# A static schedule that models its load queue: a held weight transfer, copies kept on one engine, and re-measured durations

## Chip, cores and metric

One Trainium2 chip, one core. The metric is device time in microseconds (us) of one execution. The kernel before took 300.09 to 304.71 us. A profile shows one execution, and its span is 1.7 to 1.8 us shorter than that execution's time. The profile before is of a quick execution (300.43 us, 2.9 us under the median of 303.29).

## The reference

Attention over key blocks chosen by a gate, then an MLP on its output. Types are float32 in and out.

```python
# q, k, v: (4, 8, 768, 64).  w_in: (512, 2048), w_out: (2048, 512)
k_rep = k.reshape(B, H, 12, 64, D).mean(axis=3)            # one mean key for each 64-row block
gate  = einsum('bhsd,bhnd->bhsn', q, k_rep)                # where causal, else -1e9
mask  = own block | the 3 best blocks of gate, & causal
out   = softmax(where(mask, q @ k.T / 8, -1e9)) @ v
x     = out.transpose(0, 2, 1, 3).reshape(3072, 512)
return gelu_tanh(x @ w_in) @ w_out
```

## The kernel before

Heads go in pairs: pairs 0 to 3 are batch 0, 4 to 7 batch 1, and so on to 15. A pair needs loads of k, q and v, a gate (small float32 matmuls of q with the block-mean keys), a top-3 mask that a DMA transposes, and the attention itself. A batch then needs `s1` (MLP-up: 64 pairs of 512- and 256-column matmuls, each slice followed by a gelu on ScalarE) and `s2` (MLP-down, which needs all of w_out). The order is meant to overlap one batch's MLP with the next batch's gates and loads.

All of this is described as operations with a list of possible engines, a guessed duration, and dependencies. A greedy list scheduler in Python picks an engine and a place for each, once, when the program is built. On the chip the engines work through the chosen orders and wait on each other, so a wrong guess in the model becomes an order that stalls.

```python
class Plan:                                      # the scheduler, cut to its idea
    def solve(self):
        ...
        for op in cand:
            r = op.ready                          # when its dependencies end, in the model
            for e, d in op.engines.items():       # engine -> guessed us
                s = max(r, clock.get(e, 0.0))
                ests.append((s, s + d, e, op))
        first = min(x[0] for x in ests) + self.WINDOW
        # of those that can start first: the smallest prio, then the engine that ends it soonest
        ...

def load(p, key, held=None, prio=None):           # k, q, v of pair p, all issued by SyncE
    ...
    go = add({SP: 2.0 if dve else 1.0}, emit_t if dve else emit,
             [free_sd.get((key, p - (PV if key == "v" else PF))), held],
             prio=10 * p if prio is None else prio)          # the issue
    ld[key, p] = add({"DMA": 2.5 if dve else 1.8}, lambda _: None, [go],
                     prio=1000 * b + hp, lag=1.6)            # the landing, as modelled

free_sd["v", p] = ld["v16", p] = add({DVE: 0.47, ACT: 0.8}, emit, ...)   # cast of v
...
go  = add({SP: 1.2}, mask_dma, [sel], -50)                   # mask transpose, also on SyncE
m   = add({"XBAR": 0.8}, lambda _: None, [go], pr, lag=1.7)
mcs = [add({DVE: 0.25, ACT: 0.65}, mc(h), [m, old.get("s")], pr) for h in range(2)]  # mask copies
...
add({SP: 0.1}, out_e, [cp], -50)                             # output store, also on SyncE
...
# in the main sequence, at pair 5 (HP is 4):
w_ready["out"] = load_w("out", w_out16, moe_w_out, slice(0, DM), [issued["q", HP + 1]], 30)
```

For pairs 4 to 15, k and q come in as 128-byte records, already cut for VectorE's 32x32 transposes. w_out (2 MB, issued by GpSimd) comes in as 2048 records of 1024 bytes.

Two things in the built program matter that the model before does not have. First, SyncE's transfers take turns on eight semaphores (counters by which a transfer says that it has landed), as the operands in the trace show, so none is issued before the eighth transfer before it has landed. One load of k or q is four transfers, one of v is two. Second, an issue on SyncE can itself last long ("46.44 5.85 SPq" below), and the eight semaphores are not the reason: the fourth transfer of that line is issued from 48.52 to 52.29, while the eighth before it had landed at 47.15; the next transfer, of v, from 52.39 to 57.23, while the eighth before it had landed at 47.67. Of the single issues over 2 us, five of six fall while w_in or w_out is being loaded. What holds them stays open.

The softmax here doesn't subtract the row's maximum and nothing guards it: scores larger than these inputs give would overflow.

Of the kernel before, what the change touches and what calls it, by code (L numbers as in the profile page):

```python
# [8 lines left out]
FP32 = mybir.dt.float32  # L9
# [113 lines left out]
def kernel(  # L123
# [9 lines left out]
    nc = tc.nc  # L133
# [6 lines left out]
    HP = H // 2  # L140
    NPAIR = B * HP
    PF = 4
# [68 lines left out]
    issued = {}  # L211
    free_sd = {}

    def load(p, key, held=None, prio=None):
        b, hp = divmod(p, HP)

        def emit(_):
            sd = (iov if key == "v" else io).tile(
                [128, NC, 2, 64], FP32, tag=key, name=f"{key}_sd_{p}")
            for hh in range(2):  # L220
                nc.sync.dma_start(  # L221
                    out=sd[:, :, hh, :],
                    in_=SRC[key][b, 2 * hp + hh].rearrange(
                        "(c p) d -> p c d", p=128))
            T[key, p] = sd
        def emit_t(_):

            sd = io.tile([128, NC * 4, 32], FP32, tag=key, name=f"{key}_sd_{p}")
            for hh in range(2):
                for a in range(2):  # L230
                    nc.sync.dma_start(  # L231
                        out=sd[64 * hh + 32 * a:64 * hh + 32 * a + 32],
                        in_=SRC[key][b, 2 * hp + hh].rearrange(
                            "(t i) (a j) -> a i t j", i=32, j=32)[a])
            T[key, p] = sd
        dve = key != "v" and p >= HP
        go = add({SP: 2.0 if dve else 1.0}, emit_t if dve else emit,
                 [free_sd.get((key, p - (PV if key == "v" else PF))), held],
                 prio=10 * p if prio is None else prio)
        issued[key, p] = go  # L240
        ld[key, p] = add({"DMA": 2.5 if dve else 1.8},
                         lambda _: None, [go],
                         prio=1000 * b + hp, lag=1.6)

    def cast_v(p, old):
        b, hp = divmod(p, HP)

        def emit(eng):
            copy(eng, v16[p % NB][:, :, :, 0:64], T["v", p])
        free_sd["v", p] = ld["v16", p] = add(  # L250
            {DVE: 0.47, ACT: 0.8}, emit,
# [3 lines left out]
    def load_w(name, dst, src, cols, deps, prio):  # L255
        view = src.rearrange("(i p) f -> p i f", p=128)

        def emit(_):
            nc.gpsimd.dma_start(out=dst[:, :, cols], in_=view[:, :, cols])
# [76 lines left out]
    def pre(p):  # L336
# [51 lines left out]
        else:  # L388
            t = add({DVE: 0.95}, tr("k"),
# [15 lines left out]
            kcs = [add({DVE: 0.56, ACT: 0.73}, kc_all(h),  # L405
# [32 lines left out]
        else:  # L438
            t = add({DVE: 0.95}, tr("q"),
# [25 lines left out]
        gx = add({DVE: 0.32}, gm_e, [g], pr, gives=[("gt", p)])  # L465
# [18 lines left out]
        sel = add({DVE: 1.6}, sel_e, [gx, c_E["gates"], c_E["ones", i]], pr)  # L484
# [5 lines left out]
        else:  # L490
# [5 lines left out]
            q16s = [add({DVE: 0.56, ACT: 0.75}, q16(h), qcs + [old.get("s")],  # L496
# [26 lines left out]
        else:  # L523
            go = add({SP: 1.2}, mask_dma, [sel], -50)
            m = add({"XBAR": 0.8}, lambda _: None, [go], pr, lag=1.7)
# [6 lines left out]
            mcs = [add({DVE: 0.25, ACT: 0.65}, mc(h), [m, old.get("s")], pr)  # L532
# [18 lines left out]
    def table(key, deps, prio):  # L551
        if key not in tables:
# [6 lines left out]
            tables[key] = add({ACT: 1.5}, emit, deps, prio)  # L559
# [6 lines left out]
    def heads2(p):  # L566
# [81 lines left out]
        norms = [add({DVE: 0.72}, norm(p, h), pvs[h], base - 20,  # L648
# [18 lines left out]
    def turn_out(p, norms, base):  # L667
# [23 lines left out]
        if p >= HP + 2:  # L691
            go = add({SP: 1.2}, ot_dma, norms, -50)
            x = add({"XBAR": 0.8}, lambda _: None, [go], base - 20, lag=1.7)
        else:
            ot = add({PE: 0.33}, ot_e, norms, base + 50,
                     takes=("pre", ("oT", p)))
            x = add({DVE: 0.47, ACT: 0.7}, otc_e, [ot], base - 20,
# [3 lines left out]
    def heads(p):  # L701
# [5 lines left out]
        for h in range(2):  # L707
            pvs = []
            for gi, (ja, jb) in enumerate(groups):
# [30 lines left out]
                ex = add({ACT: 0.8}, ex_e,  # L740
# [33 lines left out]
            norms.append(add({DVE: 0.72}, norm(p, h), pvs, base - 20,  # L774
# [10 lines left out]
    def s1(b):  # L785
        for f in range(NF):
# [14 lines left out]
            def ge_e(_, f=f):  # L801
# [9 lines left out]
                add({ACT: 0.7}, ge_e,  # L811
# [4 lines left out]
    def s2(b):  # L816
        kind = "ops" if b < B - 1 else "tail"
        prev = None
        for ti in range(NC):
# [18 lines left out]
            cp = add({DVE: 0.6, ACT: 0.5}, cp_e, [mm], 1000 * b + 500,  # L838
# [42 lines left out]
    for p in range(HP, NPAIR):  # L881
# [6 lines left out]
        if p == HP + 1:  # L888
            w_ready["out"] = load_w("out", w_out16, moe_w_out, slice(0, DM),
                                    [issued["q", HP + 1]], 30)  # L890
            s2(0)
# [39 lines left out]
```

## Time and profile before

| | us |
|---|---|
| median of 4 runs beside the kernel after | 303.29 (302.52 to 304.36) |
| span of the profiled execution | 298.7 |
| TensorE busy / ScalarE / VectorE | 269.9 / 185.7 / 132.0 |

TensorE is 90% busy, but not evenly. The page's second part shows the span in 40 slices of 7.5 us (tenths of busy time; PEclk is the granted clock in tenths):

```profile
PE   7999999543699887995999999999999999999995
...
PEclk9999999957699999999899999999999999999999
DMA  9995999999998999999920222740002231000111
```

The eighth to eleventh digits (52 to 82 us) are the hole, and the clock drops in the ninth to eleventh. DMA is nearly full through the first twenty: up to there the loads lag behind what the engines could eat.

The stages can be cut by ScalarE's activation-table loads (gelu of batch 0, exp of batch 1, gelu of batch 1, exp of batch 2). Before the first is stage A. This is the windows view of the kernel before (stretch, its length, busy us and count of instructions of each engine, clock, DMA share, GB/s):

```profile
45.46:91.97 46.51, 31.53 (x206) 18.32 (x203) 17.36 (x53) 21.04 (x28) 1.90 (x3) 0.82 1.23 168
91.97:126.02 34.05, 29.93 (x311) 16.84 (x309) 25.59 (x69) 28.34 (x36) 10.16 (x23) 1.00 1.07 164
126.02:162.28 36.26, 32.35 (x211) 17.14 (x209) 23.48 (x85) 23.18 (x31) 0.81 (x1) 0.95 0.78 131
162.28:298.70 136.42, 132.78 (x1031) 73.96 (x1029) 37.14 (x120) 84.68 (x109) 20.55 (x48) 1.00 0.20 55
```

Call them B (MLP-up of batch 0), C (attention of batch 1), D (MLP-up of batch 1) and E (the rest). B lasts 46.5 us with TensorE busy for 31.5 us of it at clock 0.82; it is where the time is lost.

The two longest groups of waits of TensorE, before:

```profile
PE wide L792 <- ACT gT L805: 11.0, 2, 7.3
PE bank L449 <- DVE ksb L412: 7.7, 1, 7.7
```

And the timeline of the kernel before, around those waits (start, length, engine, line, operation, what it waited for before it in brackets):

```profile
46.19 1.17 POOL L259 DMA_DIRECT2D w_out<-in_moe_w_out_dram  x1
46.44 5.85 SPq L231 DMA_DIRECT2D q_sd<-in_q_dram  x4
...
63.01 0.98 DVE L372 STREAM_TRANSPOSE qT<-q_sd 128x768 f32<-128x768 f32 x1 [8.43 <-DMA q_sd<-in_q_dram]
...
64.12 0.76 PE L449 MATMUL bank<-qT,ksb 128*32 128x160 f32 x8 [7.67 <-DVE ksb L412]
...
72.25 1.31 SPq L510 DMA_TRANSPOSE mT<-madd  x1
...
75.65 0.72 ACT L202 COPY qT<-mT 12x640 f16<-12x640 f16 x1 [10.09 <-DMA mT<-madd]
...
77.26 13.14 PE L792 MATMUL wide<-xT,w_in 128*128 128x512 f16 x72 [7.30 <-ACT gT L805]
```

Read it as two chains. First: w_out is issued at 46.19, q of pair 5 at 46.44; q is not there until 63, so VectorE waits 8.43 us, and TensorE stands at the gate of pair 5 for 7.67 us. The bracket names ksb (the block-mean keys, spread out by VectorE for the gate's matmuls) because that multiply came last, but VectorE was itself waiting for q. Second: the mask transpose of pair 4 is issued only at 72.25, behind the loads up to k of pair 7 in SyncE's queue, though its input was ready at 52.7. A mask copy that the scheduler gave to ScalarE waits for it, the gelus stand behind that copy in ScalarE's order, and TensorE waits 7.30 us for a gelu to free its PSUM buffer.

The DMA records, counted from the raw trace of the kernel before (records per 2 us):

```text
window us     w_out (1024 B)   loads (128 B)
46 - 48             0              2346
50 - 52           385                63
52 - 54           293               288
54 - 56           357               354
58 - 60           353               354
w_out runs from 48.4 to 61.5
```

From 52 to 60 us the two flows get the same number of records, so w_out gets eight times the bytes. The Trainium skill ("DMA: Bandwidth & Descriptors", Queues, rings and completion order) says that each DMA engine goes round its queue rows packet by packet. A packet of that page holds several descriptors, and the trace shows single records, so it can't show the packets; equal shares agree with the page if the packets of both flows hold equally many. The number from the trace: the loads fall from about 1,170 records per us to about 180.

### The profile page before, as it was taken

To read this page: it belongs to the slowest core of one execution; us is meant where nothing else is said; L and a number is where in the kernel's file an instruction comes from. 1 tells how busy PE (TensorE), PEld (TensorE's weight loads), DVE (VectorE), ACT (ScalarE), POOL (GpSimd) and SP (SyncE) were. 2 spreads that over 40 slices of the span, in tenths; PEclk is the share of its full clock that TensorE was granted. 3 is DMA by queue.
4 is the path that set the end of the run, shared out by engine and by line. 5 is a ranking of instruction groups with operands and counts; after the bars stand their busy time and mean duration, and the time that the engine had idled before them with its cause. 6 is when DMAs were issued, how large, how long until landed. Compare 5 with 4: busy or idle time off the path is not lost.

```text
span 298.7 us, 5866 instructions
## 1 busy us (share of the span) xinstructions
PE 269.9 (90%) x2278; PEld 157.4 (53%) x2278; DVE 132.0 (44%) x441; ACT 185.7 (62%) x240; POOL 51.3 (17%) x120
## 2 busy tenths in 40 slices
PE   7999999543699887995999999999999999999995
PEld 6976557311365454542465565456656654565442
DVE  0468888250073597896760799930003320000000
ACT  1377788420569958965667999736679951665111
POOL 8205332000001323500000454000015510000000
PEclk9999999957699999999899999999999999999999
DMA  9995999999998999999920222740002231000111
GB/s 171 219 211 97 213 146 170 200 172 154 167 161 132 190 177 152 171 200 192 162 47 2 58 52 67 169 120 0 0 2 61 64 91 70 35 2 0 70 72 70
DMA packets 135596, 33.68 MB, mean 113 GB/s; under 512 B 129424, under 2 KB 131472, under 8 KB 135568
## 3 DMA queue, kind: packets, MB, share of 16 engines
q1 hardware_dynamic: 132448, 29.11, 56.3%
q0 software_dynamic: 3120, 4.19, 8.3%
q8 instruction: 18, 0.29, 0.4%
q14 instruction: 10, 0.08, 0.1%
HBM read 27.26 MB, written 6.29 MB: 112 GB/s over the span
## 4 chain that ended last, share of the span: by engine, by line
PE 72%; DVE 7%; DMA 7%; ACT 5%; SPq 5%; issue 2%; POOL 1%; DVEq 0%; ACTq 0%; POOLq 0%
PE wide L792 25%; PE bank L823 22%; PE wide L723 7%; PE bank L857 4%; PE bank L762 4%; DMA mT<-madd 3%; PE wide L583 3%; SPq L231 3%; ACT at L736 3%; DMA v_sd<-in_v_dram 3%; SPq L221 2%; PE bank L349 2%; PE bank L636 2%; DVE mx L476 2%; PE bank L355 2%
## 5 line engine op out<-in xcount | busy, mean ns | idle before, releaser
L792 PE MATMUL wide<-xT,w_in 128*128 128x512 f16 (+1 forms) x512 | 91.2, 338 | 11.0 <-ACT gT L805 11.0
L823 PE MATMUL bank<-w_out,gT 128*128 128x512 f16 x384 | 98.1, 379 | 1.8 <-DVE gx L462 1.8
L792 PEld LDWEIGHTS <-w_in 128*128 128x128 f16 x512 | 51.2, 101 | 49.1 <-issue 17.1
L805 ACT ACTIVATE gT<-wide 128x768 f16<-128x768 f32 x64 | 51.4, 810 | 28.7 <-PE wide L792 28.5
L736 ACT ACTIVATE at<-wide 128x896 f16<-128x896 f32 x72 | 60.6, 915 | 3.5 <-PE wide L723 2.3
L750 POOL TENSOR_SCALAR_AFFINE_SELECT at<-at 128x256 f16<-128x256 f16 x72 | 31.5, 438 | 162.6 <-ACT at L736 162.3
L823 PEld LDWEIGHTS <-gT 128*128 128x128 f16 x384 | 35.8, 98 | 36.8 <-issue 3.1
L723 PE MATMUL wide<-qT,kT 76*128 76x512 f16 (+1 forms) x192 | 39.0, 305 | 1.8 <-ACT at L736 1.8
L202 ACT COPY osb<-bank 128x512 f32<-128x512 f32 x18 | 10.5, 584 | 33.7 <-PE bank L823 30.1
L762 PEld LDWEIGHTS <-at 128*128 128x128 f16 x504 | 23.8, 97 | 11.5 <-POOL at L750 3.5
L762 PE MATMUL bank<-v,at 128*128 128x65 f16 x504 | 27.2, 194 | 0.3 <-POOL at L750 0.2
L597 ACT ACTIVATE at<-wide 128x1024 f16<-128x1024 f32 (+1 forms) x24 | 20.7, 917 | 4.3 <-PE wide L583 4.1
L723 PEld LDWEIGHTS <-kT 76*128 76x128 f16 x192 | 15.5, 98 | 12.5 <-issue 2.4
L857 PE MATMUL bank<-ident 128*128 128x256 f16 x110 | 16.9, 291 | 1.8 <-DVE ident L166 1.8
L662 DVE TENSOR_TENSOR xn<-bank,zr 128x384 f16<-128x384 f32 x32 | 17.8, 558 | 1.1
L206 DVE COPY qT<-mT 12x640 f16<-12x640 f16 x18 | 6.0, 335 | 25.9 <-DMA mT<-madd 25.7
L206 DVE COPY osb<-bank 128x512 f32<-128x512 f32 x6 | 4.1, 687 | 26.4 <-PE bank L823 26.4
L372 DVE STREAM_TRANSPOSE qT<-q_sd 128x768 f32<-128x768 f32 x12 | 11.6, 965 | 8.4 <-DMA q_sd<-in_q_dram 8.4
L202 ACT COPY qT<-mT 12x640 f16<-12x640 f16 x6 | 4.3, 722 | 17.2 <-DMA mT<-madd 17.2
L449 PE MATMUL bank<-qT,ksb 128*32 128x160 f32 x128 | 7.5, 320 | 7.7 <-DVE ksb L412 7.7
L476 DVE MAX8 mx<-gm 128x8 f32<-128x12 f32 x160 | 13.2, 157 | 0.6
L623 POOL TENSOR_SCALAR_AFFINE_SELECT at<-at 128x256 f16<-128x256 f16 (+1 forms) x16 | 8.7, 559 | 26.4 <-ACT at L597 26.4
(72 smaller groups left out, 218.7 us busy)
## 6 DMA issues: line engine op xcount, KB each, us to landing
v_sd<-in_v_dram SPq DMA_DIRECT2D x32, 192.0 KB, 4.1
out_dram<-osb SPq DMA_DIRECT2D x24, 256.0 KB, 2.2
k_sd<-in_k_dram SPq DMA_DIRECT2D x48, 96.0 KB, 3.8
q_sd<-in_q_dram SPq DMA_DIRECT2D x48, 96.0 KB, 3.5
w_in<-in_moe_w_in_dram POOLq DMA_DIRECT2D x2, 1024.0 KB, 11.0
w_out<-in_moe_w_out_dram POOLq DMA_DIRECT2D x1, 2048.0 KB, 16.0
k_sd<-in_k_dram SPq DMA_DIRECT2D x8, 192.0 KB, 4.4
q_sd<-in_q_dram SPq DMA_DIRECT2D x8, 192.0 KB, 4.3
```

The lines of the kernel that those rows point to most:

```text
L202: nc.scalar.copy(out=out, in_=in_)
L476: nc.vector.max(out=mx8[:, x, :], in_=gm[:, x, :])
L597: nc.scalar.activation(out=T["at", u][:, :, 0:n], in_=plan.buf[("st",) + u].rearrange("p (h w) -> p h w", h=2)[:, :, 0:n], func=AF.Exp, bi ...
L662: nc.vector.tensor_tensor(out=T["xn", p][:, :, h, :], in0=pvv[:, :, 0:64], in1=zr.to_broadcast([128, NC, 64]), op=ALU.mult)
L723: nc.tensor.matmul(st[:, x:e], kT16[i][h][0:76, s0:s0 + 128], qT16[i][h][0:76, s0 + (x - cb):s0 + (e - cb)], start=True, stop=True)
L736: nc.scalar.activation(out=T["at", u][:, 0:n], in_=plan.buf[("st",) + u][:, 0:n], func=AF.Exp, bias=0.0, scale=SCALE)
L750: nc.gpsimd.affine_select(out=dg, in_=dg, compare_op=ALU.is_ge, fill=0.0, base=0, pattern=[[0, 2], [1, 128]], channel_multiplier=-1)
L762: nc.tensor.matmul(pvv[:, qc, 0:65], at[:, cb + (qc - jc) * 128: cb + (qc - jc + 1) * 128], v16[i][:, jc, h, :], start=(gi == 0 and jc == ...
L792: nc.tensor.matmul(hps[:, u:e], w_in16[:, ci, f * 128:(f + 1) * 128], T["xT", b][:, ci, u:e], start=(ci == 0), stop=(ci == HP - 1))
L805: nc.scalar.activation(out=T["gT", b][:, f, :], in_=plan.buf["hps", b, f][:, 0:S], func=AF.Gelu_apprx_tanh, bias=0.0, scale=1.0)
L823: nc.tensor.matmul(plan.buf["ops", b, ti], T["gT", b][:, f, ti * 128:(ti + 1) * 128], w_out16[:, f, :], start=(f == 0), stop=(f == NF - 1))
L857: nc.tensor.matmul(plan.buf["warm", n][:, 0:256], ident16, z, start=True, stop=True)
```

## The change

The intent: let the scheduler know what the queue does, so that the order it picks is one that the chip can follow.

- Back-pressure: a load may be issued, in the model, only when the third load before it has landed (`moved[-3:-2]`, some eight transfers).
- w_out is held: a 16-element copy on GpSimd reads v of pair 5, and the transfer follows it on GpSimd.
- v casts and mask copies go to VectorE only.
- The guessed durations and the lag of DMA transposes are set closer to measured ones.

No arithmetic changes and no work is added but that copy.

```diff
@@ def load
         go = add({SP: 2.0 if dve else 1.0}, emit_t if dve else emit,
-                 [free_sd.get((key, p - (PV if key == "v" else PF))), held],
+                 [free_sd.get((key, p - (PV if key == "v" else PF))), held]
+                 + moved[-3:-2],
...
+        moved.append(ld[key, p])
@@ def cast_v
-            {DVE: 0.47, ACT: 0.8}, emit,
+            {DVE: 0.47}, emit,
@@ def load_w
+            if after is not None:
+                x = const.tile([1, 16], FP32, name="after")
+                nc.gpsimd.tensor_copy(out=x, in_=T[after][0:1, 0, 0, 0:16])
             nc.gpsimd.dma_start(out=dst[:, :, cols], in_=view[:, :, cols])
@@ mask transpose and its copies
-            m = add({"XBAR": 0.8}, lambda _: None, [go], pr, lag=1.7)
+            m = add({"XBAR": 0.8}, lambda _: None, [go], pr, lag=2.5)
...
-            mcs = [add({DVE: 0.25, ACT: 0.65}, mc(h), [m, old.get("s")], pr)
+            mcs = [add({DVE: 0.33}, mc(h), [m, old.get("s")], pr)
@@ s1: one of the other changed durations
-                add({ACT: 0.7}, ge_e,
+                add({ACT: 0.81}, ge_e,
@@ main sequence
-                                    [issued["q", HP + 1]], 30)
+                                    [ld["v", HP + 1]], 30, ("v", HP + 1))
```

More of the change, by code (lines that the diff above doesn't have):

```diff
@@ L211 @@
     issued = {}
+    moved = []
     free_sd = {}
@@ L250, in cast_v, with load_w @@
         free_sd["v", p] = ld["v16", p] = add(
-            {DVE: 0.47, ACT: 0.8}, emit,
+            {DVE: 0.47}, emit,
             [ld["v", p], old],
             prio=1000 * (b - 1) + 599 + hp if b else 100 * hp - 55)
-    def load_w(name, dst, src, cols, deps, prio):
+    def load_w(name, dst, src, cols, deps, prio, after=None):
         view = src.rearrange("(i p) f -> p i f", p=128)
         def emit(_):
+            if after is not None:
+                x = const.tile([1, 16], FP32, name="after")
+                nc.gpsimd.tensor_copy(out=x, in_=T[after][0:1, 0, 0, 0:16])
             nc.gpsimd.dma_start(out=dst[:, :, cols], in_=view[:, :, cols])
@@ L388, in pre @@
         else:
-            t = add({DVE: 0.95}, tr("k"),
+            t = add({DVE: 0.98}, tr("k"),
                     [ld["k", p], last.get(p - 2, {}).get("k32")], pr)
@@ L404, in kc_all @@
                 return emit
-            kcs = [add({DVE: 0.56, ACT: 0.73}, kc_all(h),
+            kcs = [add({DVE: 0.56, ACT: 0.84}, kc_all(h),
                        [t, old.get("k", None)], pr + 0.1) for h in range(2)]
@@ L438, in pre @@
         else:
-            t = add({DVE: 0.95}, tr("q"),
+            t = add({DVE: 0.98}, tr("q"),
                     [ld["q", p], last.get(p - 3, {}).get("pre")], pr)
@@ L464, in gm_e @@
                 in_=plan.buf["gt", p][:, 0:160])
-        gx = add({DVE: 0.32}, gm_e, [g], pr, gives=[("gt", p)])
+        gx = add({DVE: 0.36}, gm_e, [g], pr, gives=[("gt", p)])
         def sel_e(_):
@@ L483, in sel_e @@
                 in1=T["ownm1"], op0=ALU.add, op1=ALU.max)
-        sel = add({DVE: 1.6}, sel_e, [gx, c_E["gates"], c_E["ones", i]], pr)
+        sel = add({DVE: 1.72}, sel_e, [gx, c_E["gates"], c_E["ones", i]], pr)
         if first:
@@ L495, in q16 @@
                 return emit
-            q16s = [add({DVE: 0.56, ACT: 0.75}, q16(h), qcs + [old.get("s")],
+            q16s = [add({DVE: 0.56, ACT: 0.84}, q16(h), qcs + [old.get("s")],
                         pr + 0.1) for h in range(2)]
@@ L558, in emit @@
                     bias=0.0, scale=1.0)
-            tables[key] = add({ACT: 1.5}, emit, deps, prio)
+            tables[key] = add({ACT: 1.45}, emit, deps, prio)
         return tables[key]
@@ L647, in heads2 @@
                                   takes=("pv", ("pv", p, h))))
-        norms = [add({DVE: 0.72}, norm(p, h), pvs[h], base - 20,
+        norms = [add({DVE: 0.78}, norm(p, h), pvs[h], base - 20,
                      gives=[("pv", p, h)]) for h in range(2)]
@@ L692, in turn_out @@
             go = add({SP: 1.2}, ot_dma, norms, -50)
-            x = add({"XBAR": 0.8}, lambda _: None, [go], base - 20, lag=1.7)
+            x = add({"XBAR": 0.8}, lambda _: None, [go], base - 20, lag=2.5)
         else:
@@ L696, in turn_out @@
                      takes=("pre", ("oT", p)))
-            x = add({DVE: 0.47, ACT: 0.7}, otc_e, [ot], base - 20,
+            x = add({DVE: 0.56, ACT: 0.8}, otc_e, [ot], base - 20,
                     gives=[("oT", p)])
@@ L739, in ex_e @@
                         func=AF.Exp, bias=0.0, scale=SCALE)
-                ex = add({ACT: 0.8}, ex_e,
+                ex = add({ACT: 0.84}, ex_e,
                          [st, table(("exp", b), gelus.get(b - 1, []), base)],
@@ L772, in heads @@
                                pr, takes=("pv", ("pv", p, h))))
-            norms.append(add({DVE: 0.72}, norm(p, h), pvs, base - 20,
+            norms.append(add({DVE: 0.78}, norm(p, h), pvs, base - 20,
                              gives=[("pv", p, h)]))
@@ L837, in cp_e @@
                 copy(eng, osb, plan.buf["ops", b, ti])
-            cp = add({DVE: 0.6, ACT: 0.5}, cp_e, [mm], 1000 * b + 500,
+            cp = add({DVE: 0.69, ACT: 0.58}, cp_e, [mm], 1000 * b + 500,
                      gives=[("ops", b, ti)])
```

## The prediction

> **What bounds the kernel now.** Cut into stages (windows view, span 298.7 us): first batch 0-45.5; MLP-up of batch 0, 45.5-92; attention of batch 1, 92-126; MLP-up of batch 1, 126-161.4; the rest, 137.3 us. From 161.4 on TensorE is never idle until the drain. The loss lies before: MLP-up of batch 0 has 64 pairs of matmuls that take 20.2 us in batch 2 (chain of waits), but lasts 46.5 us here. TensorE idles 56.4-64.1 (gate of pair 5 <- ksb, 7.7 us) and 69.9-77.3 (<- gelu on ScalarE, 7.3 us), and the clock is halved around both (stretches of 0.52 and 0.66). Causes:
> - w_out is issued at 46.2 and its 2 KB packets hold the DMA engines from about 48 to 61 (DMA records). The 128-byte packets of q of pair 5 fall from about 1100 to about 180 per us in that time; q of pair 5 lands near 62.9. The Trainium skill ("DMA: Bandwidth & Descriptors", Queues, rings and completion order) says that an engine round-robins between queue rows by packet, which agrees with small packets losing.
> - The mask transpose of pair 4 is issued only at 72.25, behind six loads in SyncE's queue, though its input was ready at 52.7; a mask copy on ScalarE waits for it till 75.65 and holds the gelus.
> The same in small later: ScalarE waits for mask or load in 105-113 (about 5 us) and 131-147 (gelus 0 to 4 of batch 1 come over 11 us).
>
> **What the change moves** (instruction order of both kernels). No work is added but one 16-element POOL copy. SyncE: each mask transpose comes before the next loads (pair 4 after k of pair 6, pair 8 before k of pair 11, pair 11 before k of pair 14); the transposes of pairs 6 and 7 come before k of pair 12. But the first output store now stands before q of pair 8. ScalarE loses 6 v casts (0.83 us each) and 6 mask copies (0.72); VectorE gains them at about 0.55 and 0.33: about 9.3 us off ScalarE, of which only some 3 us lies in attention of batch 1, where ScalarE bounds. TensorE: the gate of pair 6 moves ahead, to 20 matmul pairs after the gate of pair 5.
>
> **Cost of it.** Without w_out, q and v of pair 5 follow at 2.3 us a load: v lands near 54.5, gate of pair 5 near 56. w_out then runs about 56.5-69.5, and now it is q of pair 6, issued near 55, that starves, till about 71. TensorE runs its 20 pairs (6.4 us) and stands at the gate of pair 6 from about 62.5 to 73-74, with the clock halved again. So two stalls become one of about 11 us; attention of batch 1 starts near 85.5, not 92: **-6.5 us** (with no stall it would be about -17). Loads after pair 6 land at nearly the old times, as DMA is saturated, and VectorE and ScalarE meet no mask wait: attention of batch 1 about 29.5 us (**-4.5**), MLP-up of batch 1 about 29 (**-6**). The last 137 us stay. Sum -17 us: **286 us**, range 278 to 293. Chances: faster 0.91, same 0.07, slower 0.02.
>
> **What would show it.** One idle stretch of 8-12 us at the gate of pair 6, ended by q of pair 6; none at pair 5 and none from mask to gelu; w_out landing near 70; the mask transpose of pair 4 near 54; ScalarE stalls in attention of batch 1 under 2 us; the last stage 136-139 us.
>
> **What would make it wrong.** Upward gain: q of pair 6 gets through before w_out starts (about 277). Downward: the first output store in SyncE's queue holds loads of pair 8 long enough to move gates of batch 2 late; VectorE's in-order mask copies hold norms and so PSUM.

## The result

| | before | after |
|---|---|---|
| median, us | 303.29 | 290.02 (288.37 to 290.31) |
| ratio, 95% interval | | 0.9549 (0.9499 to 0.9598) |
| span of the profile, us | 298.7 | 288.1 |
| TensorE / ScalarE / VectorE busy | 269.9 / 185.7 / 132.0 | 268.4 / 180.9 / 134.4 |

A ratio here and below is the mean time of one kernel's fast runs over that of the kernel before in the same rounds, so it is not quite the ratio of the medians quoted.

The 40 slices, after:

```profile
PE   7999999990799999949999999999999999999994
...
PEclk9999999997599999997999999999999999999998
DMA  8991999999873999999994332460011321000111
```

The hole of four digits is now one of two (a 0, then a 7), and there is a second, small one at the eighteenth digit. The windows view after, cut by the same four table loads (columns as before):

```profile
46.38:85.36 38.98, 29.10 (x207) 17.21 (x204) 22.77 (x75) 21.12 (x28) 2.23 (x4) 0.87 1.01 167
85.36:115.41 30.05, 30.05 (x330) 17.50 (x329) 20.59 (x63) 27.98 (x37) 10.44 (x24) 1.00 0.84 149
115.41:150.10 34.69, 30.96 (x181) 16.59 (x179) 23.03 (x73) 21.00 (x28) 0.00 (x0) 0.95 0.99 183
150.10:288.10 138.00, 134.12 (x1035) 74.08 (x1033) 40.01 (x125) 82.44 (x104) 20.59 (x48) 0.99 0.24 59
```

| stage, us | A | B | C | D | E |
|---|---|---|---|---|---|
| before | 45.5 | 46.5 | 34.0 | 36.3 | 136.4 |
| after | 46.4 | 39.0 | 30.0 | 34.7 | 138.0 |

B gives 7.5 us and C gives 4.0; D, which is 36 us long, gives 1.6. In C TensorE is now busy without a gap (30.05 of 30.05).

The waits of TensorE, after: the line that stands for both groups of before (the wait for a gelu is gone from the list):

```profile
PE bank L455 <- DVE ksb L418: 13.6, 2, 9.9
```

Two stalls, 9.88 us and 3.73 us. The timeline of the kernel after shows the first one, in B:

```profile
52.82 0.33 POOL L264 COPY after<-v_sd 1x16 f32<-1x16 f32 x1 [5.66 <-DMA v_sd<-in_v_dram]
...
53.10 1.17 POOL L265 DMA_DIRECT2D w_out<-in_moe_w_out_dram  x1
...
54.91 3.28 SPq L516 DMA_TRANSPOSE mT<-madd  x1
...
58.30 10.98 SPq L232 DMA_DIRECT2D q_sd<-in_q_dram  x4
...
68.76 0.65 DVE L206 COPY qT<-mT 12x640 f16<-12x640 f16 x2 [8.51 <-DMA mT<-madd]
...
71.63 0.98 DVE L378 STREAM_TRANSPOSE qT<-q_sd 128x768 f32<-128x768 f32 x1 [1.22 <-DMA q_sd<-in_q_dram]
...
74.06 0.76 PE L455 MATMUL bank<-qT,ksb 128*32 128x160 f32 x8 [9.88 <-DVE ksb L418]
```

w_out starts 7 us later and lets pair 5 through; then q of pair 6 starves, its four transfers issued over 10.98 us, and TensorE stands at the gate of pair 6. The mask transpose of pair 4 is issued early, at 54.91, but starves too: it lands 13.8 us later, and VectorE waits 8.51 us for it. Only then, after a transpose of k, does it wait 1.22 us more for q. So the two victims share this stall: with q in time and the mask as late, it would be about 1.2 us shorter (an estimate from these two waits). The counted records say the same:

```text
kernel after, records per 2 us
window us     w_out (1024 B)   128 B   256 B (v)
58 - 60           260           136       0
60 - 62           347           346       0
62 - 64           363           286      64
64 - 66           299             0     299
68 - 70            54          2253       0
w_out runs from 55.0 to 69.0
```

The second stall is in D, in the same timeline:

```profile
81.15 2.47 SPq L232 DMA_DIRECT2D k_sd<-in_k_dram  x4
90.40 0.38 SPq L848 DMA_DIRECT2D out_dram<-osb  x1
90.81 2.25 SPq L232 DMA_DIRECT2D q_sd<-in_q_dram  x4
...
123.44 0.57 ACT L202 COPY osb<-bank 128x512 f32<-128x512 f32 x1
...
124.40 0.47 SPq L848 DMA_DIRECT2D out_dram<-osb  x1
...
124.97 1.24 SPq L516 DMA_TRANSPOSE mT<-madd  x1
...
127.86 0.65 DVE L206 COPY qT<-mT 12x640 f16<-12x640 f16 x2 [1.58 <-DMA mT<-madd]
128.52 0.19 DVE L418 TENSOR_TENSOR ksb<-bmask,ks 128x32 f32<-128x32 f32 x1
...
128.77 0.48 PE L455 MATMUL bank<-qT,ksb 128*32 128x160 f32 x8 [3.73 <-DVE ksb L418]
```

Read the last six lines upwards: the gate of pair 11 waits for ksb, which stands behind the mask copies of pair 9 in VectorE's order, which wait 1.58 us for a mask transpose. Its input was ready at 119.44, but in SyncE's queue it stood behind a transpose of the attention output, k of pair 12 (issued until 124.30) and an output store. That store did not wait for its PSUM copy, which had ended at 124.01. The first three lines are the same queue earlier: SyncE issues k of pair 8 until 83.6, then nothing for 6.8 us, because the next in its order is an output store that is not ready until 90.40. q of pair 8 waits behind it.

D had a stall before, too, and of the same length. It is the second of the two waits for a gelu in the list above, again behind a mask copy on ScalarE:

```profile
141.71 3.26 PE L792 MATMUL wide<-xT,w_in 128*128 128x512 f16 x10 [3.69 <-ACT gT L805]
```

So in D one stall of 3.7 us stands in place of another, and TensorE is idle in it for 3.9 us before and 3.7 after. What D lost is busy time of TensorE (32.35 to 30.96): 181 of its matmuls lie there, and not 211.

### The profile page after: what moved, and what is told of

Its sections match the earlier page's. It is cut to its first block, busy times and chain, and to the rows that moved or that the text cites. A ratio compares the mean times of both kernels' runs of the same rounds, so it can differ in the third digit from the quotient of the medians.

```text
span 288.1 us, 5862 instructions
## 1 busy us (share of the span) xinstructions
PE 268.4 (93%) x2278; PEld 157.3 (55%) x2278; DVE 134.4 (47%) x449; ACT 180.9 (63%) x232; POOL 51.4 (18%) x121
## 2 busy tenths in 40 slices
DMA packets 135596, 33.68 MB, mean 117 GB/s; under 512 B 129424, under 2 KB 131472, under 8 KB 135568
## 4 chain that ended last, share of the span: by engine, by line
PE 79%; SPq 5%; DVE 5%; DMA 5%; ACT 3%; issue 2%; POOL 1%; DVEq 0%; ACTq 0%; POOLq 0%
PE wide L798 26%; PE bank L829 24%; PE wide L729 8%; PE bank L768 5%; PE bank L863 5%; SPq L232 4%; PE wide L589 4%; DMA mT<-madd 2%; PE bank L355 2%; PE bank L642 2%; PE bank L455 2%; PE bank L361 2%; DMA q_sd<-in_q_dram 2%; ACT at L742 1%; SPq L516 1%
## 5 line engine op out<-in xcount | busy, mean ns | idle before, releaser
L829 PE MATMUL bank<-w_out,gT 128*128 128x512 f16 x384 | 99.5, 379 | 0.0
L798 PE MATMUL wide<-xT,w_in 128*128 128x512 f16 (+1 forms) x512 | 89.0, 334 | 0.0
L811 ACT ACTIVATE gT<-wide 128x768 f16<-128x768 f32 x64 | 51.4, 809 | 35.2 <-PE wide L798 35.2
L742 ACT ACTIVATE at<-wide 128x896 f16<-128x896 f32 x72 | 61.8, 914 | 5.0 <-PE wide L729 2.0
L202 ACT COPY osb<-bank 128x512 f32<-128x512 f32 x19 | 11.1, 582 | 32.4 <-PE bank L829 31.9
L729 PEld LDWEIGHTS <-kT 76*128 76x128 f16 x192 | 18.2, 97 | 15.1 <-issue 0.2
L455 PE MATMUL bank<-qT,ksb 128*32 128x160 f32 x128 | 7.9, 321 | 13.6 <-DVE ksb L418 13.6
L863 PE MATMUL bank<-ident 128*128 128x256 f16 x110 | 18.3, 303 | 1.8 <-DVE ident L166 1.8
L206 DVE COPY qT<-mT 12x640 f16<-12x640 f16 x24 | 7.8, 324 | 21.0 <-DMA mT<-madd 20.8
L202 ACT CAST kT<-kT 64x768 f16<-64x768 f32 x13 | 10.8, 829 | 9.0 <-DVE kT L378 8.9
L206 DVE COPY osb<-bank 128x512 f32<-128x512 f32 x5 | 3.4, 689 | 27.0 <-ACT at L742 18.7
L667 DVE RECIPROCAL zr<-bank 128x6 f32<-128x6 f32 x32 | 6.1, 190 | 19.3 <-PE bank L768 17.8
L863 PEld LDWEIGHTS <-ident 128*128 128x128 f16 x110 | 11.4, 110 | 4.8 <-DVE ident L166 1.8
```

The costliest lines, as they stand in the source:

```text
L202: nc.scalar.copy(out=out, in_=in_)
L455: nc.tensor.matmul(g[32 * j:32 * j + 32, 0:160].rearrange("g (c t) -> g c t", t=32), T["ksb", p].rearrange("p h n -> p (h n)"), q5[:, j], ...
L729: nc.tensor.matmul(st[:, x:e], kT16[i][h][0:76, s0:s0 + 128], qT16[i][h][0:76, s0 + (x - cb):s0 + (e - cb)], start=True, stop=True)
L742: nc.scalar.activation(out=T["at", u][:, 0:n], in_=plan.buf[("st",) + u][:, 0:n], func=AF.Exp, bias=0.0, scale=SCALE)
L798: nc.tensor.matmul(hps[:, u:e], w_in16[:, ci, f * 128:(f + 1) * 128], T["xT", b][:, ci, u:e], start=(ci == 0), stop=(ci == HP - 1))
L811: nc.scalar.activation(out=T["gT", b][:, f, :], in_=plan.buf["hps", b, f][:, 0:S], func=AF.Gelu_apprx_tanh, bias=0.0, scale=1.0)
```

## The experiments

All twelve kernels gave correct results. Theory 1, from the prediction: the gain is that B has one stall instead of two. Theory 2: D gained little because output stores stand before loads and transposes in SyncE's order. The rivals were that single parts of the change carry it alone, and that the loads as a whole are the limit.

A stage ends where a table load stands, so work can cross its border: between kernels whose order differs, compare the sum of B, C and D, or what TensorE is idle for in a stage. The medians of e7 and e10 are of all four runs; one run of e7 (297.7) and two of e10 count as slow and are not in the ratios.

| run | ratio (95%) | median, us | A | B | C | D | E |
|---|---|---|---|---|---|---|---|
| after | 0.9549 (0.9499-0.9598) | 290.0 | 46.4 | 39.0 | 30.0 | 34.7 | 138.0 |
| e1 back-pressure alone | 0.9691 (0.9661-0.9721) | 293.0 | 46.5 | 38.9 | 28.8 | 39.7 | 138.1 |
| e2 hold alone | 0.9817 (0.9789-0.9845) | 296.7 | 46.7 | 45.6 | 26.9 | 38.3 | 137.5 |
| e3 VectorE only, alone | 0.9840 (0.9796-0.9883) | 297.9 | 45.6 | 37.3 | 40.1 | 35.0 | 138.0 |
| e4 durations alone | 0.9887 (0.9839-0.9934) | 298.8 | 45.5 | 45.2 | 32.6 | 36.0 | 136.3 |
| e5 after, no back-pressure | 0.9770 (0.9741-0.9799) | 294.7 | 46.1 | 45.0 | 30.0 | 34.4 | 137.7 |
| e6 after, no hold | 0.9739 (0.9703-0.9774) | 293.2 | 46.9 | 39.2 | 30.8 | 39.0 | 137.3 |
| e7 hold for q of pair 6 | 0.9574 (0.9525-0.9624) | 289.1 | 45.7 | 40.3 | 27.2 | 35.2 | 137.7 |
| e8 w_out right after w_in | 0.9448 (0.9425-0.9471) | 284.8 | 46.6 | 26.7 | 40.5 | 32.5 | 136.9 |
| e9 stores on GpSimd | 0.9489 (0.9444-0.9534) | 286.7 | 46.8 | 38.8 | 29.9 | 30.9 | 139.2 |
| e10 model of starvation (stages of a slow run) | 0.9323 (0.9252-0.9395) | 284.2 | 45.6 | 37.1 | 31.9 | 34.1 | 137.1 |
| e11 w_out in 256-byte records | 0.9484 (0.9423-0.9544) | 286.6 | 46.8 | 35.9 | 30.0 | 35.2 | 138.0 |
| e12 e9's stores, hold for mask 4, modelled | 0.9415 (0.9377-0.9453) | 285.0 | 46.6 | 28.4 | 32.4 | 38.6 | 139.2 |

### Each part alone: e1 to e4

e1 adds only `moved[-3:-2]` to the kernel before:

```diff
-                 [free_sd.get((key, p - (PV if key == "v" else PF))), held],
+                 [free_sd.get((key, p - (PV if key == "v" else PF))), held]
+                 + moved[-3:-2],
+        moved.append(ld[key, p])
```

> Before plus only the modelled back-pressure of the load queue. Theory A (the gain comes from mask transposes that no longer stand behind loads in SyncE's queue): 290 to 295 us; TensorE's 7.3 us wait for a gelu held by a mask copy is gone, the 7.7 us wait at the gate of pair 5 (q of pair 5 starved by w_out) stays, attention of batch 1 is about 30 us long instead of 34. Theory B (holding w_out carries the gain): 299 to 303 us. Theory C (taking copies off ScalarE carries it): 301 to 303 us.

It gave 3.1%, within the range of theory A, and is the largest of the four. B is already as short as in the kernel after (38.9 against 39.0), though the gate of pair 5 still stalls for 8.5 us: the order puts the mask transposes early, and the wait for a gelu in B is gone. C is shorter by the same means: with as many matmuls as before (312 and 311) TensorE is idle in it for 0.2 us instead of 4.1. But D is 39.7, longer than before, with a wait of 5.5 us for a gelu.

e2 holds w_out and changes nothing else:

```diff
-                                    [issued["q", HP + 1]], 30)
+                                    [ld["v", HP + 1]], 30, ("v", HP + 1))
+                nc.gpsimd.tensor_copy(out=x, in_=T[after][0:1, 0, 0, 0:16])
```

> Before plus only the hold of w_out till v of pair 5 has landed. Theory A: the starvation only moves to pair 6, with one stall of 8 to 12 us at its gate, and the mask transpose of pair 4 still stands behind k of pair 7 and so behind the starved load, so gelus are still held by its copy: 297 to 304 us. Theory B: 290 to 294 us. Theory C: 301 to 303 us.

It gave 1.8% (just under the 297 us of theory A), and hardly any of it in B (45.6 against 46.5). C is shorter (26.9 against 34.0), in part because 31 of its 311 matmuls have moved elsewhere. The one stall was foretold for the gate of pair 6; it came at a gelu. The timeline of this run shows why: without back-pressure in the model the mask transpose of pair 4 still stands behind the loads, and the one stall becomes the other.

```profile
71.06 1.30 SPq L513 DMA_TRANSPOSE mT<-madd  x1
...
73.78 0.72 ACT L202 COPY qT<-mT 12x640 f16<-12x640 f16 x1 [14.56 <-DMA mT<-madd]
...
75.39 1.23 PE L795 MATMUL wide<-xT,w_in 128*128 128x512 f16 x3 [14.58 <-ACT gT L808]
```

The gate of pair 5 no longer waits, and ScalarE waits 14.56 us for the mask instead.

e3 takes ScalarE out of the two copies:

```diff
-            {DVE: 0.47, ACT: 0.8}, emit,
+            {DVE: 0.47}, emit,
-            mcs = [add({DVE: 0.25, ACT: 0.65}, mc(h), [m, old.get("s")], pr)
+            mcs = [add({DVE: 0.25}, mc(h), [m, old.get("s")], pr)
```

> Before plus only mask and v copies on VectorE alone. Theory A and B: both stalls of TensorE in MLP-up of batch 0 stay or nearly (the second may shrink as ScalarE's gelus no longer stand behind a mask copy: then 296 to 300), 298 to 303 us. Theory C: 292 to 296 us, with ScalarE busy 9 us less and attention of batch 1 4 us shorter.

At 297.9 us it is where theories A and B put a shrunken second stall. It frees the gelus in B (37.3 us, the shortest of the four; left is one stall of 8.8 us at the gate of pair 5) but gives most of that back in C (40.1 against 34.0), where two gates wait 4.7 us for ksb and 4.5 us for a q that came late.

e4 changes the durations only, with the copies still allowed on ScalarE:

```diff
-            m = add({"XBAR": 0.8}, lambda _: None, [go], pr, lag=1.7)
+            m = add({"XBAR": 0.8}, lambda _: None, [go], pr, lag=2.5)
-                add({ACT: 0.7}, ge_e,
+                add({ACT: 0.81}, ge_e,
# and the others of the diff
```

> Before plus only the other durations (and the longer lag of transposes). All theories: within 1.5% of before, 299 to 306 us, both stalls of MLP-up of batch 0 present. A different result would say that the order is sensitive to small numbers of the model and that the parts cannot be added up.

It gave 1.1%, just outside the range on record. The waits stay: 8.7 us for gelus and 7.8 for ksb.

Alone the four give 9.3, 5.5, 4.8 and 3.4 us (each from its ratio and the mean of about 302.3 of the kernel before in those rounds), 23 together; the change as a whole gives 13.7 in the same way. So the parts are not additive. No interval of the four reaches 1. The stage table shows one reason: e1 and e3 both bring B to 37-39 us by freeing the same gelus, and the change can have that only once.

### The change without one part: e5 and e6

```diff
# e5: the kernel after, without the back-pressure
-                 [free_sd.get((key, p - (PV if key == "v" else PF))), held]
-                 + moved[-3:-2],
+                 [free_sd.get((key, p - (PV if key == "v" else PF))), held],
```

> The changed kernel without the modelled back-pressure. If the parts substitute for each other (the mask copies on VectorE alone already free the gelus): 290 to 295 us, the stall at the gate of pair 6 grows to about 13 us because the transposes of k and q of pair 6 stand behind the mask copy of pair 4 on VectorE, whose transpose stands behind k of pair 7. If the parts add: 290 + 9 = 299 us.

It landed in the range for parts that substitute for each other. Taking the back-pressure away costs 2.2 points of ratio, all in B (45.0 against 39.0). The stall at the gate of pair 6 is 13.6 us long instead of 9.88, as foretold. C has the same length, but TensorE is idle in it for 2.9 us again.

```diff
# e6: the kernel after, without the hold of w_out
-                                    [ld["v", HP + 1]], 30, ("v", HP + 1))
+                                    [issued["q", HP + 1]], 30)
```

> The changed kernel with w_out issued at the old place. Theory A (the hold only moves the starvation from pair 5 to pair 6): 288 to 293 us, one stall of 8 us at the gate of pair 5 instead of the 9.9 us at the gate of pair 6. If the hold carries its own 5.5 us (as it did alone): 295 us.

Taking the hold away costs 1.9 points, and none of it in B: 39.2 against 39.0. The stall is back at the gate of pair 5, 9.0 us long, in place of the 9.88 us at pair 6. In B the hold only chooses which load starves. Its worth lies in D (39.0 against 34.7): here TensorE waits there 3.8 us for transposes of the attention output and 3.6 us at a gate. In the order of this kernel the first output store stands before k of pair 8, one load earlier than in the kernel after. That the position of the stores makes this difference is argued from the order and not shown; e9, below, does not settle it. The median (293.2) is just over the range of theory A.

### Where w_out can go: e7, e8, e11

e7 holds w_out until q of pair 6 has landed, which is the load that starved:

```diff
-        if p == HP + 1:
+        if p == HP + 2:
-                                    [ld["v", HP + 1]], 30, ("v", HP + 1))
+                                    [ld["q", HP + 2]], 30, ("q", HP + 2))
```

> The changed kernel with w_out held one load group longer, till q of pair 6 has landed. If w_out's packets starving q of pair 6 cause the 9.9 us stall: the gate of pair 6 stalls under 2 us, attention of batch 1 starts at 74 to 78 us instead of 85.4, w_out lands near 75 to 78 and TensorE waits for it a few us: 281 to 286 us. If the stall has another cause (the order of VectorE, the mask transpose): 288 to 291 us.

The gate of pair 6 now runs at 63.58 without a stall, as foretold. The time did not follow (0.9574; C starts at 86.05 and not at 74 to 78), for the same reason as ever; the timeline of this run:

```profile
58.62 10.89 SPq L232 DMA_DIRECT2D k_sd<-in_k_dram  x4
...
76.11 0.67 DVE L206 COPY qT<-mT 12x640 f16<-12x640 f16 x2 [11.64 <-DMA mT<-madd]
...
79.52 0.83 ACT L202 CAST kT<-kT 64x768 f16<-64x768 f32 x1 [10.97 <-DVE kT L378]
...
81.11 1.23 PE L798 MATMUL wide<-xT,w_in 128*128 128x512 f16 x3 [10.80 <-ACT gT L811]
```

Now k of pair 7 starves, and the mask transpose of pair 5 stands behind it in SyncE's queue. VectorE waits 11.64 us for that mask and transposes k only after it (k had landed by 75.5). ScalarE's copy of k waits 10.97 us, the gelus stand behind that copy, and TensorE waits 10.80 us.

e8 moves w_out to where no pair's load competes: right after w_in, with the loads of pair 4 held till w_out has landed.

```diff
-    held = hold(w_ready["in", 0])
+    w_ready["out"] = load_w("out", w_out16, moe_w_out, slice(0, DM),
+                            [ld["v", 2]], 32)
+    held = hold(w_ready["out"])
```

> The changed kernel with w_out issued right after w_in and the loads of pair 4 on held till it has landed, so that no small packets share the engines with it. If the starvation is the cost: no gate stall over 3 us in MLP-up of batch 0, 278 to 286 us. If the engines' total time is the cost (all loads come 13 us later): MLP-up of batch 0 runs through but attention of batch 1 waits for its loads, 287 to 292 us.

The stall in B is gone: 26.7 us. But all loads of batch 1 come later, and C takes 40.5 us, so each of the two expectations is right in part. The longest waits of TensorE in this run are small ones:

```profile
PE wide L798 <- DMA xT<-xn: 3.7, 1, 3.7
PE wide L729 <- DVE qT L206: 3.1, 1, 3.1
```

B and C together are 67.1 us against 69.0 in the kernel after; D is 32.5. At 284.8 us it beats both kernels, with the narrowest spread of all (284.61 to 285.12).

e11 leaves w_out where the change put it and cuts it into four transfers of 128 columns, so that its records are 256 bytes:

```diff
-            nc.gpsimd.dma_start(out=dst[:, :, cols], in_=view[:, :, cols])
+            step = 128 if after is not None else cols.stop - cols.start
+            for c in range(cols.start, cols.stop, step):
+                nc.gpsimd.dma_start(out=dst[:, :, c:c + step],
+                                    in_=view[:, :, c:c + step])
```

> The changed kernel with w_out moved by four transfers of 128 columns each, so in packets of a quarter of the size, with the same order of instructions. If a load's share beside w_out is set by the size of w_out's packets: q of pair 6 moves at 400 to 700 packets per us instead of 180, lands near 62 to 66 instead of 71.5, the stall at the gate of pair 6 falls from 9.9 to 2 to 5 us, and w_out takes 18 to 26 us instead of 17: 284 to 288 us. If w_out holds the engines whatever its packet size: the stall stays 9 us or more, 289 to 293 us.

```text
records per 2 us, e11
window us     w_out (256 B)   128 B
61 - 63          1093           863
63 - 65          1121          1116
65 - 67          1220           783
w_out runs from 56.0 to 74.5
```

```profile
71.24 0.76 PE L458 MATMUL bank<-qT,ksb 128*32 128x160 f32 x8 [6.65 <-DVE ksb L421]
```

Where the flows share fully (63 to 65 us) they again get the same number of records, but a record of w_out is now a quarter as long, and the loads get 390 to 560 records per us in these windows where they got at most 173 in the kernel after. VectorE has q of pair 6 at 68.81 instead of 71.63, and the stall at its gate is 6.65 us instead of 9.88. w_out takes 18.5 us instead of 14. B is 3.1 us shorter. This is the direct test that share goes by count of records: the traces of the two kernels have the same order on TensorE and ScalarE, and on SyncE and VectorE all but the same. The stall was foretold at 2 to 5 us, so the size was missed. In time, the intervals of e11 and of the kernel after overlap.

### The output stores: e9

```diff
-                nc.sync.dma_start(out=out_rows[b * NC + ti],
+                nc.gpsimd.dma_start(out=out_rows[b * NC + ti],
                                   in_=T["osb", b, ti])
-            add({SP: 0.1}, out_e, [cp], -50)
+            add({POOL: 1.2}, out_e, [cp], -50)
```

> The changed kernel with the output stores issued by POOL, so that none stands in SyncE's queue ahead of loads. If the stores in SyncE's queue cause the second stall (gate of pair 11, 3.7 us, and the clock after it): the 8.7 us gap in SyncE before q of pair 8 is gone, MLP-up of batch 1 is 29 to 31 us instead of 34.7, the first stall of 10 us stays: 283 to 287 us. If the second stall has another cause (VectorE's in-order mask copies): 288 to 291 us.

The timeline of this run, at the place where the kernel after has SyncE idle:

```profile
80.63 2.46 SPq L232 DMA_DIRECT2D k_sd<-in_k_dram  x4
83.13 3.68 SPq L232 DMA_DIRECT2D q_sd<-in_q_dram  x4
```

q of pair 8 is issued straight after k. The text calls the old gap 8.7 us; the trace of the kernel after shows 6.8 (83.6 to 90.40). B stays as it was (38.8, stall at the gate of pair 6 9.1 us), D falls from 34.7 to 30.9, and the gate of pair 11 does not wait. That is what theory 2 asks for, but it doesn't show it, for the scheduler also found another order:

```profile
126.65 3.73 PE L798 MATMUL wide<-xT,w_in 128*128 128x512 f16 x22 [0.25 <-ACT gT L811]
130.31 0.48 PE L455 MATMUL bank<-qT,ksb 128*32 128x160 f32 x8
```

The gate of pair 11 now stands behind 34 matmuls of s1 that follow the gate of pair 10, where 12 stood in the kernel after. It runs later (130.31 against 128.77), and its ksb comes later too (129.23 against 128.52). What took the stall away is this order. The old gap of 6.8 us can hardly have caused it: with and without it, the gates of pairs 7 to 10 run within 0.3 us of the same times, and SyncE has a gap of 6.2 us in e9 as well (90.38 to 96.62). Whether the stores in SyncE's queue cost D anything stays open. E is 1.2 us longer, the intervals of e9 and of the kernel after overlap, and issued from GpSimd the stores also go in fewer records (134,060 in all against 135,596).

### The models of starvation: e10 and e12

e10 adds no work and changes only the model: every load of pair 6 and later, but for k of pair 6, is taken to land after w_out, so that the scheduler itself knows of the starvation.

```diff
-                         lambda _: None, [go],
+                         lambda _: None,
+                         [go, w_ready.get("out") if (p, key) != (HP + 2, "k")
+                          else None],
```

> The changed kernel with one more edge in the scheduler alone: the loads behind k of pair 6 land after w_out has landed, as the traces show; no instruction or transfer is added, the gate of pair 6 goes behind the matmuls of MLP-up of batch 0. If the 9.9 us stall is the scheduler's belief that q of pair 6 passes w_out: MLP-up of batch 0 takes 26 to 29 us instead of 39; part of it comes back in attention of batch 1, whose loads come no earlier: 36 to 41 us; 280 to 286 us. If TensorE is bound by the landing itself: attention waits for all of it and the time stays 288 to 291 us.

The gate of pair 6 moved behind all remaining 44 matmul pairs of s1, and its stall went. This kernel's times scatter: 280.72, 282.59, 285.71 and 287.44, of which the last two count as slow. The ratio of 0.9323, the lowest of all, rests on two runs, and neither has a profile. Whether the scatter is the chip's slower state or this kernel's own is open: the granted clock of its slow runs (0.975 and 0.981) is that of other kernels' fast ones. The times of the fast runs are in the range; the foretold B of 26 to 29 us is not seen. The profile is of a slow one, so it is read only for its chain and not for lengths beside other runs:

```profile
53.76 3.26 SPq L518 DMA_TRANSPOSE mT<-madd  x1
...
67.73 0.67 DVE L206 COPY qT<-mT 12x640 f16<-12x640 f16 x2 [8.30 <-DMA mT<-madd]
...
69.44 0.83 ACT L202 CAST kT<-kT 64x768 f16<-64x768 f32 x1 [7.83 <-DVE kT L380]
...
71.03 1.22 PE L800 MATMUL wide<-xT,w_in 128*128 128x512 f16 x3 [7.67 <-ACT gT L813]
```

What starves now is the mask transpose of pair 4, which the model of e10 did not count among the starving: VectorE waits 8.30 us for it, k of pair 6 is transposed behind it, ScalarE's copy of k follows, and the gelus behind that. In the kernel after the same wait of VectorE (8.51 us) came first, and that for q added 1.22 us.

e12 puts together what helped: stores on GpSimd, w_out held until the mask transpose of pair 4 has landed, and in the model the loads from v of pair 6 on, and the mask transposes, land after w_out.

```diff
-            m = add({"XBAR": 0.8}, lambda _: None, [go], pr, lag=2.5)
+            m = add({"XBAR": 0.8}, lambda _: None,
+                    [go, w_ready.get("out")], pr, lag=2.5)
+            landed[p] = m
...
+        if p == HP:
+            w_ready["out"] = load_w("out", w_out16, moe_w_out, slice(0, DM),
+                                    [landed[HP]], 30, ("mT", HP))
# and e9's two lines for the stores, and a condition like e10's in load
```

> The changed kernel with three things: w_out waits for the landing of the mask transpose of pair 4 instead of v of pair 5 (so that this transpose, starved till 67 to 69 us in the traces, and q of pair 6 get through first), the scheduler knows that loads and mask transposes issued behind w_out land after it, and POOL issues the output stores. If starvation beside w_out and the stores ahead of loads are what is left of the two stalls: no stall of TensorE over 3 us, MLP-up of batch 0 26 to 30 us, attention of batch 1 30 to 34, MLP-up of batch 1 30 to 33: 275 to 281 us. If the loads as a whole bound the stretch from 46 to 150 us (their landing is no earlier): what is won in MLP-up of batch 0 comes back in attention of batch 1, over 36 us: 283 to 287 us.

The large stalls in B are gone: B is 28.4 us, against 39.0. But the time stops at 285.0 (six runs, 284.46 to 286.83), level with e8 and over the 281 us hoped for. TensorE waits 4.1 us for w_out itself, in C, and 3.9 us for transposes of the attention output, in D. D is 38.6 with 222 matmuls in it, where the kernel after has 181. Add up B, C and D: 116.8 us before, 103.7 after, and 99.7, 99.6 and 99.4 in e8, e9 and e12. Three quite different orders end at the same sum, each with its stalls elsewhere. That fits the rival, that the loads as a whole set this stretch: in e8 and e12 the DMA row of the page stands at 9 in nearly every slice of it. But e9 has one slice there at 2, the rival's own sign for e12 (C over 36 us) did not come (32.4), and the fast runs of e10 speak against a floor at this sum: their spans are 279.0 and 280.9 us, which leaves about 96 and 98 us for B, C and D if A and E are as long as in its profile (an estimate). The agreement may be chance. The limit is argued, not shown, and stays open: no run here makes the loads themselves cheaper, which is what would test it.

## Why the prediction was right, and where it was off

The prediction was 286 us (278 to 293); the median is 290.02. Point by point:

- **Two stalls become one, of 8 to 12 us, at the gate of pair 6: right.** 9.88 us, ended by q of pair 6 (after a longer wait of VectorE for the mask, see the third point); none at pair 5, whose gate ran at 57.08 (predicted 56). w_out landed about 70 (predicted 70), q of pair 6 at 71.2 to 71.6 (predicted 71). Attention of batch 1 started at 85.36, against 85.5 predicted: 6.6 us of the 6.5 foretold. e6, e7 and e11 confirm the mechanism: moved, w_out starves pair 5, pair 6 or pair 7; cut into smaller records, it starves less. What made B short is the other half of it: with one stall of 8.5 to 9.9 us, B is 37 to 39 us in e1, e3, e6 and the kernel after, whether w_out is held or not; with two stalls, or one of 13.6 us or more, it is 45 to 46.5 (before, e2, e4, e5).
- **"its 2 KB packets": wrong in a detail.** The records of w_out are of 1024 bytes; 2 KB is the length of its rows in the source, before the cast to 16 bits.
- **"VectorE and ScalarE meet no mask wait": wrong.** The mask transpose of pair 4 was issued at 54.91 as foretold, but starved beside w_out like a load (13.8 us to land, where the usual one takes about 3). Of VectorE's waits before the gate of pair 6, 8.51 us were for this mask and 1.22 for q, which came later still. In e10 it was what bound.
- **Attention of batch 1, -4.5 us: right.** 34.0 to 30.0, with ScalarE's waits there at 1.8 us (predicted under 2).
- **MLP-up of batch 1, -6 us: the mis-sized term.** 36.3 to 34.7, so -1.6. The prediction counted on no mask wait in D. There still was one: TensorE's stall of 3.69 us (a gelu behind a mask copy on ScalarE) gave way to one of 3.73 us at the gate of pair 11 (ksb behind mask copies on VectorE), and each comes with 3.4 us of half clock. The text had named VectorE's in-order mask copies, and the store before q of pair 8, among the things that could make it wrong, and gave them no us. That store held q of pair 8 for 6.8 us, with no cost that the traces show. In e9 D drops to 30.9 with the stall gone, but by another order of TensorE, so the cost of the stores stays open.
- **ScalarE loses 9.3 us: half of it came back.** The 12 copies left, but its busy time fell by 4.8 us (185.7 to 180.9): the scheduler gave it four more copies of q and one more PSUM copy in exchange, and one copy of k fewer. When an engine is made free in a list scheduler's model, the scheduler fills it.
- **The last stage stays: off by 1.6 us.** 138.0 against 136.4, inside the predicted 136 to 139; TensorE's busy time there rose from 132.8 to 134.1. This was not followed up.

The terms: predicted -6.5 - 4.5 - 6 + 0 = -17; measured in the spans -6.6 - 4.0 - 1.6 + 1.6 = -10.6. Of the difference of 6.4 us, 4.4 is D. The timed medians differ by 13.3, so the total came out closer than the sum of the stages. That is luck: the profile before, from which the stages were cut, is of an execution 2.9 us quicker than the median.

The clock, which the prediction counted in with the stalls: the Trainium skill ("TensorE: Matmul & The Clock Gate", What's actually happening) says that TensorE's clock is halved after an idle window of about 3.4 us and restored after about as much busy time, by windows that run freely. The traces agree in the main: before, the clock fell at 59.4, 3.0 us after TensorE went idle, and stayed low till 69.65, 5.5 us after it had resumed; after, it was low from 68.1 to 78.4. But for the last, at the end of the program, the stretches of half clock last 10.24, 6.83 or 3.41 us, whole numbers of windows of 3.41 us. Before, B pays 10.24 and 6.83 us of half clock, after, only 10.24. In D each kernel has 3.41 us of it.

## What to carry to other kernels

A static schedule is only as good as its model of the queues: a load that waits for the transfers before it, a transpose that stands behind the loads before it, and a large transfer that starves small records all have to be in the model, or the engines' fixed orders turn them into stalls of work that had nothing to do with them. In these runs a big transfer with long records beside many short ones took its share by count of records, so delaying it only chose the next victim; put it where nothing competes, cut its records, or keep what must not wait out of its way. Do not add up the gains of scheduling changes measured one at a time, and when a changed model makes a stall go away, look whether the cause went or only the order changed: in e9 the operand came later than before and the stall was gone.

## What the Trainium skill lacked or had wrong

- "DMA: Bandwidth & Descriptors" (Queues, rings and completion order) says that an engine goes round its queue rows by packet. It does not say what that does to bytes. In these runs (which show records, and not that page's packets) two flows got the same number of records (347 and 346 in 2 us), so a transfer with 1024-byte records took eight times the bytes of one with 128-byte records, whose rate fell from about 1,170 to about 180 records per us. With 256-byte records in the large transfer the small ones kept 390 to 560 per us.
- The same page (Issuing engines are not separate DMA queues) says that issuing from several engines saves only the sequencer's time to initiate, "which is usually small relative to the DMA itself". The page has, in another section (Anatomy of one DMA), that a wait for a semaphore is held on the issuing engine, but does not say what this means for the choice of that engine: here a store that was not ready held a load behind it for 6.8 us, and the issue of a single transfer lasted up to 4.84 us (kernel before).
- The same page (DMA Transpose (X-bar)) gives constraints and hazards but no time for a small transpose within SBUF ("VectorE: DVE Perf Modes", The three transpose paths, has 1309 ns for one of 128x128, and does not say if that counts the landing). Here those of the mask mostly took about 3 us to land, with an issue of about 1.2 us on SyncE; beside w_out one took 13.8 us to land and 3.28 us to issue.
- "TensorE: Matmul & The Clock Gate" (What's actually happening) does not say how idle a window must be to halve the clock, or how busy to restore it. On the grid of 3.41 us in these two traces, five windows at full clock with 0 to 0.81 us of matmul time were followed by half clock, and none from B to D with 2.13 us or more was; at half clock 2.64 us were enough to restore it and 2.12 us were not.
